# Narrowing doubles in two VectorE passes, and column sums in 64-column products

## The chip, the cores and the metric

The kernel runs on one core of a Trainium2 chip. A core has five engines that run side by side and meet through semaphores: TensorE (PE, matrix products into PSUM; its weight loads are listed as PEld), VectorE (DVE), ScalarE (ACT), GpSimd (POOL) and SyncE (SP, which here only issues transfers). The metric is the device time of one execution in microseconds; the median of the runs counts.

## The reference

Two blocks follow one another. The first is an attention with sketched polynomial features, for 4 batches, 4 heads, 1088 positions and 32 dimensions; the second is a feed-forward block with a sigmoid gate on 4352 tokens of 128 features, with 1536 hidden features.

```
phi(x):  a = x S1^T, b = x S2^T          # 8 values each
         phi = outer(a, b) as 64 features
q_p, k_p = phi(q), phi(k)
kv  = sum over s of k_p[s] v[s]^T        # 64 x 32
z   = sum over s of k_p[s]               # 64
x   = (q_p kv) / (q_p z + 1e-6)          # heads side by side: 4352 x 128

gate = sigmoid(x @ w_gate)               # 128 x 1536
out  = (gate * (x @ w_val)) @ w_out      # 1536 x 128
```

q, k and v come as 32-bit floats. [...]

## The kernel before

**Stages.** Until about 15 us the kernel builds the features of batch 0 and the first rows of x (transposed, tile `xT`). Then it goes through the tokens in chunks of 512 (`tok_chk`, nine chunks, the last of 256). For each chunk, `w1` makes one "wave" per block j of 128 hidden features (12 blocks, `NJ`): two products of `xT` with w_gate and w_val (line 501), a sigmoid on ScalarE (line 509) and, one slot later, the multiplication `g` on VectorE (line 540). `w2` (line 382) sums chunk 0 through w_out; chunks 1 to 7 use a scheme of seven half-size products (`w2_a`, `w2_b`, line 338) that needs sums of g, made by GpSimd (line 328). The attention of batches 1 to 3 is woven between the waves.

**Order.** All engines but SP follow an order written out by hand: instructions go to each engine's queue in the order of the program. `slot(group, waves)` emits a group of instructions and then that many waves, each preceded by the `glu` of the wave before and by the w2 work that is due. In chunk 0, TensorE's order is wave j, the output sum of block j−1, wave j+1, and so on.

**Narrowing.** A double is loaded as two 32-bit words, `lo` and `hi`. `narrow` is a generator of four steps. Before the change they are:

- step 0: GpSimd caps `hi`, read as a float, at ±122880 (line 97, tile `cap`); ScalarE scales `lo` to a small integer (line 101, tile `tail`);
- step 1: VectorE shifts and masks (line 105), then combines with the sign bits (line 109), giving `head`;
- step 2: ScalarE squares `cap` (line 117), into a PSUM bank of the pool `pso` where one is free; GpSimd adds `tail` to `head` as integers (line 118);
- step 3: VectorE multiplies `head` by "square is at least a threshold" (line 127), which sends tiny numbers to zero, and writes the weight into `w_sb`.

`narrow_01(part, step)` does this for blocks 0 and 1: part 0 and part 1 are gate and value of blocks 0 and 1, and part 2 is w_out of both, each of 256 columns. `narrow_w(j, step)` does blocks 2 to 11, each of 384 columns. The steps of a block are spread over the waves of chunk 0: the wave of block j emits step 3 of block j+1, steps 1 and 2 of block j+2, and step 0 of block j+4. S1 and S2 go through the same steps in a small tile of 16 partitions, at the start.

**The head.** Before the first wave: `turn_k` transposes k, `st` transposes S, `kps` and `ab` (lines 630 and 737) multiply k and q with S, `kab` (line 640) turns the result, `outer` (line 709) forms the features, `kv0` sums them with v, `dn(0, 0, rest)` makes denominators (line 1020) and numerators (line 1039), and `divide` writes `xT` (line 1060) in two parts of 256 tokens. Between them stand `warm` products of ones (line 260), whose results nobody reads. In `divide`, `between=head1` is emitted after the first transposed reciprocal `rb` (line 1070) and ahead of the first xT part.

**Denominators of batches 1 to 3.** `den_j` (line 978) makes `PD` in SBUF; `den_i` (line 991) sums it over i with a 0/1 mask of 32 columns per head, in four products; `turn_den` transposes the result (line 1003).

Of the kernel before, what the change touches and what calls it, by code (L numbers as in the profile page):

```python
# [8 lines left out]
F32 = mybir.dt.float32  # L9
I32 = mybir.dt.int32  # L10
U32 = mybir.dt.uint32
I64 = mybir.dt.int64
ALU = mybir.AluOpType
ACTF = mybir.ActivationFunctionType
MUL = ALU.mult

P = 128
# [3 lines left out]
def kernel(  # L21
# [12 lines left out]
    nc = tc.nc  # L34

    B, H, S, D = q.shape
# [4 lines left out]
    NJ = DFF // P  # L41
# [10 lines left out]
    const = ctx.enter_context(tc.tile_pool(name="const", bufs=1))  # L52
# [9 lines left out]
    pso = ctx.enter_context(tc.tile_pool(name="pso", bufs=1, space=bass.MemoryType.PSUM))  # L62
# [17 lines left out]
    wide = S1.dtype == I64  # L80
    assert all((a.dtype == I64) == wide for a in (S2, moe_w_gate, moe_w_val, moe_w_out))

    def narrow(out, bits, eng, bank=None, copies=None):

        p, n, m = bits.shape[:3]
        lo, hi = bits[:, :, :, 0].bitcast(U32), bits[:, :, :, 1]

        def tmp(dt, tag, bufs):
            return sbN.tile([P, 3, P], dt, tag=tag, name=tag, bufs=bufs)[:p, :n, :m]

        cap, tail = tmp(I32, "cap", 6), tmp(I32, "tail", 5)
        eng.tensor_scalar(
            out=cap.bitcast(F32), in0=hi.bitcast(F32), scalar1=122880.0, scalar2=-122880.0,
            op0=ALU.min, op1=ALU.max,
        )  # L100
        nc.scalar.activation(out=tail, in_=lo, func=ACTF.Copy, scale=2.0**-29)
        yield

        head = tmp(I32, "head", 3)
        nc.vector.tensor_scalar(  # L105
            out=head, in0=cap, scalar1=3, scalar2=0x3FFFFFF8,
            op0=ALU.logical_shift_left, op1=ALU.bitwise_and,
        )
        nc.vector.scalar_tensor_tensor(  # L109
            out=head, in0=cap, scalar=-0x40000000, in1=head, op0=ALU.bitwise_and, op1=ALU.bitwise_or  # L110
        )
        yield
        square = cap.bitcast(F32)
        if bank:
            square = pso.tile([P, 512], F32, tag=bank, name="square")[:, : n * m]
            square = square.rearrange("p (n m) -> p n m", n=n)
        nc.scalar.activation(out=square, in_=cap.bitcast(F32), func=ACTF.Square)
        nc.gpsimd.tensor_tensor(out=head, in0=head, in1=tail, op=ALU.add)  # L118
        yield

        head = head.bitcast(F32)
        if copies:
            square, head = (
                bass.AP(tensor=x.tensor, offset=x.offset, ap=[list(x.ap[0]), [0, copies], [1, m]])
                for x in (square, head)
            )
        nc.vector.scalar_tensor_tensor(  # L127
            out=out, in0=square, scalar=1.265625 * 2.0**-30, in1=head, op0=ALU.is_ge, op1=MUL
        )
        yield  # L130


    s4 = const.tile([2 * R, 4, D], F32, tag="s4", name="s4")
    s_in = const.tile([2 * R, 1, D, 2], I32, tag="s_in", name="s_in") if wide else s4[:, :1]
# [10 lines left out]
    w_sb = const.tile([P, 3, NJ, P], F32, tag="w_sb", name="w_sb")  # L145
    HALF = TCH // 2
    ws = const.tile([P, 4, NJ // 2, 64], F32, tag="ws", name="ws")
    w_in = {}
# [26 lines left out]
    narrowing = {}  # L175

    def narrow_w(j, step):
        if not 0 <= j < NJ:
            return
        n, jj = divmod(j, 2)  # L180
        if wide:
            if step == 0:
                narrowing[j] = narrow(
                    w_sb[:, :, j, :], w_in[n][:, :, jj], nc.gpsimd, "acc1" if j < NJ - 2 else None
                )
            next(narrowing[j])


    def narrow_01(part, step):
        if wide:  # L190
            if step == 0:
                i = (slice(0, 2), part) if part < 2 else (2, slice(0, 2))
                narrowing["01", part] = narrow(
                    w_sb[:, i[0], i[1]],
                    w_in[0][:, i[0], i[1]],
                    nc.gpsimd,
                    "acc0" if part else "acc1",
                )
            next(narrowing["01", part])


# [53 lines left out]
    def warm(*cols):  # L255
        t = psm.tile([P, 2, 512], F32, tag="wave", name="warm")
        x = nc.const_aps.tensor(1.0, [P, P], F32)
        for n in cols:
            r = nc.const_aps.tensor(1.0, [P, n], F32)
            nc.tensor.matmul(out=t[:, 0, :n], lhsT=x, rhs=r, start=True, stop=True)  # L260
# [18 lines left out]
    for c in range(2):  # L279
        rows = slice(64 * c, 64 * c + 64)  # L280
        nc.vector.tensor_reduce(
            out=m_col[rows, c],
            in_=ident[rows].rearrange("p (k j) -> p j k", j=R),
            axis=mybir.AxisListType.X,
            op=ALU.add,
        )
    for t, x in (
# [5 lines left out]
        out=e_sum,  # L293
        in_=bass.AP(
            tensor=e_row.tensor,
            offset=e_row.offset,
            ap=[list(e_row.ap[0]), [0, 2], [1, R], [0, R]],
        ),
    )
    eps = const.tile([P, 1], F32, tag="eps")  # L300
    nc.gpsimd.memset(eps, 1e-6)
    zb = const.tile([P, H, 32], F32, tag="zb", name="zb")
    nc.gpsimd.memset(zb, 0.0)
    nc.gpsimd.memset(v_sb[64:, :, 0], 0.0)
# [310 lines left out]
    KP, QP, BQ, ND, KAB, ASB, KVZ, KVD, Z4, ZS, A8, B8, ZW, PD, RC = ({} for _ in range(15))  # L615

    WD = 160
    mask = {}
# [248 lines left out]
    def kvd(b):  # L867
        KVD[b] = sbA.tile([P, 2, 2, F], F32, tag="kvd", name="kvd")
        k0 = KVZ[b][:, : 2 * F]
        n = 2 if b > 0 else 1  # L870
        nc.scalar.copy(
            out=KVD[b][:, :n],
            in_=bass.AP(
                tensor=k0.tensor, offset=k0.offset, ap=[list(k0.ap[0]), [F, n], [0, 2], [1, F]]
            ),
        )
# [19 lines left out]
    def ndt(b):  # L896
        if b == 0:
            t = pso.tile([P, TCH], F32, tag="acc0", name="ndps")
            ndps = t.rearrange("p (w x) -> p w x", w=2)
        else:  # L900
            ndps = ps2.tile([P, 2, 512], F32, tag="two", name="ndps")[:, 0].rearrange(
                "p (w x) -> p w x", w=2
            )
        if b == 0:
            nc.tensor.matmul(
                out=ndps[:, 0, :P],
                lhsT=KVD[b][:, 0].rearrange("p c f -> p (c f)"),
                rhs=ident,
                is_transpose=True,
                start=True,  # L910
                stop=True,
            )
        for c in range(2 if b else 0):
            nc.tensor.matmul(
                out=ndps[64 * c : 64 * c + 64, 0, :P],
                lhsT=KVD[b][:, 0, c],
                rhs=ident,
                start=True,
                stop=True,
            )  # L920
        ND[b] = sbA.tile([P, P], F32, tag="nd", name="nd")
        nc.scalar.copy(out=ND[b], in_=ndps[:, 0, :P])
# [64 lines left out]


    def den_i(b, dps):
        for h in range(H):  # L990
            nc.tensor.matmul(
                out=dps[32 * h : 32 * h + 32],
                lhsT=mask["head"][:, h % 2, :],
                rhs=PD[b][:, h // 2, :],
                start=True,
                stop=True,
            )
        return dps
# [85 lines left out]
        return divide  # L1084

    if wide:
        steps = narrow(s4, s_in, nc.vector, copies=4)
        for _ in range(3):
            next(steps)
    turn_k(0, 0, KBASE[2] + 1)  # L1090
# [2 lines left out]
    else:  # L1093
        nc.vector.tensor_copy(
            out=s4[:, 1:],
            in_=bass.AP(
                tensor=s4.tensor, offset=s4.offset, ap=[list(s4.ap[0]), [0, 3], [1, D]]
            ),
# [5 lines left out]
        out=st_[:, : 2 * R],  # L1104
        lhsT=s4.rearrange("p g d -> p (g d)"),
        rhs=ident[: 2 * R, : 2 * R],
# [1 line left out]
        start=True,  # L1108
        stop=True,
    )  # L1110
    warm(256)
    st_ = st_[:, : 2 * R].rearrange("p (n r) -> p n r", n=2)
    sk = const.tile([P, 2, 2, R], F32, tag="sk")
    nc.vector.tensor_tensor(
        out=sk,
        in0=bass.AP(
            tensor=st_.tensor, offset=st_.offset, ap=[list(st_.ap[0]), [0, 2], [R, 2], [1, R]]
        ),
        in1=bass.AP(
            tensor=hm.tensor, offset=hm.offset, ap=[list(hm.ap[0]), [R, 2], [0, 2], [1, R]]  # L1120
        ),
        op=MUL,
# [6 lines left out]
    for n, inner in enumerate(([[1, R], [0, R]], [[0, R], [1, R]])):  # L1129
# [3 lines left out]
            out=t, in_=bass.AP(tensor=s0.tensor, offset=s0.offset, ap=[list(s0.ap[0])] + inner)  # L1133
# [23 lines left out]
    def rest(turn, rc, dT):  # L1157
        kv0([1, 2, 3, 4, 0])
        for pi in range(2):
            outer(0, pi, 5, NJK - 1)  # L1160
        kv0(range(5, NJK))
        turn()
        nt = rc.shape[1] - 1
        nc.scalar.activation(out=rc[:, :nt], in_=dT[:, :nt, :2], func=ACTF.Identity, bias=eps)
        kvd(0)
        narrow_01(0, 1)
        narrow_01(0, 2)
        ndt(0)

    divide = dn(0, 0, rest)  # L1170
    warm(256)

    def head1():
        narrow_01(1, 1)
        narrow_01(0, 3)
        narrow_01(1, 2)
        narrow_01(2, 0)
        narrow_w(2, 0)

    divide((0, 4), (4, 8), between=head1)  # L1180
    narrow_01(1, 3)
    narrow_01(2, 1)
    narrow_01(2, 2)

# [174 lines left out]
```

## Time and profile before

| what | us |
|---|---|
| median of 3 runs | 293.81 |
| lowest and highest | 293.73 and 299.78 |
| the profiled execution | 294.1 |
| its span, first to last instruction | 292.3 |
| TensorE busy | 286.5 |
| VectorE busy | 188.8 |
| GpSimd busy | 162.7 |
| ScalarE busy | 92.1 |

The span is shorter than the time by 1.8 us, which lie around it. An engine counts as busy while one of its instructions runs. In a timeline a line has the start, the duration, the engine, the line of the program, the operation, output and inputs, and in brackets how long the engine had been idle and what it had waited for. TensorE computes a 32-bit product in two instructions.

### The profile page before, as it was taken

What the parts mean: (1) busy time and instruction counts of PE and PEld (TensorE: products, weight loads), DVE (VectorE), ACT (ScalarE), POOL (GpSimd) and SP (SyncE); (2) the same over time, 40 slices, a digit from 0 to 9 for tenths busy, and PEclk for the clock granted to TensorE, in tenths of its full rate; (3) what the DMA queues carried; (4) which work ended last, traced back from release to release, by engine and by line L of the source; (5) the groups of instructions that cost most, each with busy time, mean ns of one, the idle gap of its engine ahead of it and who ended that gap; (6) DMA issues with size and microseconds to landing.
All of it is one profiled execution on the core that took longest, in us unless ns stands there. A gap on an engine that the chain in (4) does not pass through costs nothing.

```text
span 292.3 us, 5784 instructions
## 1 busy us (share of the span) xinstructions
PE 286.5 (98%) x2276; PEld 154.9 (53%) x2276; DVE 188.8 (65%) x320; ACT 92.1 (32%) x168; POOL 162.7 (56%) x221
## 2 busy tenths in 40 slices
PE   8899999999999999999999999999999999999995
PEld 4444433345455455554555555554555555555895
DVE  6998789985837866677556685668336423642482
ACT  3557542322323222323233213423233222322421
POOL 2365644896646558546446597664465555656300
PEclk9999999999999999999999999999999999999999
DMA  7994522374720187506000584202000200010002
GB/s 216 336 354 87 147 70 84 109 185 111 239 33 0 30 195 148 147 7 183 8 0 2 153 151 108 36 2 37 0 2 0 36 2 0 0 30 8 2 2 54
DMA packets 28890, 24.23 MB, mean 83 GB/s; under 512 B 18560, under 2 KB 24064, under 8 KB 28864
## 3 DMA queue, kind: packets, MB, share of 16 engines
q1 hardware_dynamic: 25808, 21.95, 29.6%
q10 hardware_dynamic: 3056, 1.92, 2.3%
q8 instruction: 18, 0.29, 0.4%
q14 instruction: 8, 0.07, 0.1%
HBM read 20.60 MB, written 3.26 MB: 82 GB/s over the span
## 4 chain that ended last, share of the span: by engine, by line
PE 85%; DMA 6%; DVE 3%; POOL 2%; SPq 1%; issue 1%; ACT 0%; POOLq 0%; ACTq 0%
PE wave L501 55%; PE prod L338 22%; DMA v<-in_v_dram 3%; POOL head L118 2%; DMA w_in<-in_moe_w_out_dram 2%; PE moeout L408 2%; PE moeout L382 1%; PE kvz L849 1%; DVE w_sb L127 1%; DVE head L109 1%; DMA kq<-in_k_dram 1%; PE nps L1214 1%; SPq L157 1%; DVE head L105 1%; PE kps L630 1%
## 5 line engine op out<-in xcount | busy, mean ns | idle before, releaser
L501 PE MATMUL wave<-xT,w_sb 128*64 128x512 f32 (+3 forms) x820 | 210.6, 566 | 0.1
L501 PEld LDWEIGHTS wave<-xT,w_sb 128*64 128x64 f32 (+1 forms) x820 | 85.2, 140 | 63.4 <-issue 49.5
L540 DVE TENSOR_TENSOR g<-wave,sg 128x512 f32<-128x512 f32 x96 | 65.9, 686 | 77.3 <-ACT sg L509 76.2
L509 ACT ACTIVATE sg<-wave 128x512 f32<-128x512 f32 x102 | 61.0, 598 | 170.5 <-PE wave L501 161.0
L328 POOL TENSOR_TENSOR tsum<-g 128x256 f32<-128x256 f32 x84 | 68.1, 813 | 25.6 <-DVE g L540 25.2
L328 POOL TENSOR_TENSOR tsum<-g,tsum 128x256 f32<-128x256 f32 x42 | 35.2, 839 | 59.5 <-DVE g L540 59.2
L338 PE MATMUL prod<-tsum,ws 128*64 128x256 f32 x252 | 62.8, 381 | 0.0
L338 PEld LDWEIGHTS prod<-tsum,ws 128*64 128x64 f32 x252 | 31.2, 136 | 16.8 <-issue 12.4
L338 PE MATMUL prod<-g,w_sb 128*64 128x256 f32 x168 | 34.9, 383 | 0.0
L328 POOL TENSOR_TENSOR tsum<-tsum,g 128x256 f32<-128x256 f32 x42 | 32.9, 782 | 3.3
L338 PEld LDWEIGHTS prod<-g,w_sb 128*64 128x64 f32 x168 | 15.7, 136 | 18.2 <-issue 15.4
L338 PE MATMUL prod<-tsum,w_sb 128*64 128x256 f32 x84 | 25.3, 383 | 0.0
L338 PE MATMUL prod<-g,ws 128*64 128x256 f32 x84 | 25.0, 379 | 0.0
L118 POOL TENSOR_TENSOR head<-head,tail 128x384 int32<-128x384 int32 (+2 forms) x14 | 13.3, 953 | 17.9 <-DVE head L109 11.5
L338 PEld LDWEIGHTS prod<-g,ws 128*64 128x64 f32 x84 | 11.5, 137 | 3.7
L382 PE MATMUL moeout<-g,w_sb 128*128 128x512 f32 (+1 forms) x28 | 12.6, 607 | 0.3 <-DVE w_sb L127 0.3
L338 PEld LDWEIGHTS prod<-tsum,w_sb 128*64 128x64 f32 x84 | 10.8, 137 | 2.4 <-issue 1.9
L709 DVE TENSOR_TENSOR kp<-kab 128x1152 f32<-128x1152 f32 (+2 forms) x10 | 10.9, 1103 | 0.0
L829 DVE TENSOR_TENSOR qp<-qp,bq 128x1152 f32<-128x1152 f32 (+1 forms) x7 | 9.5, 1353 | 1.9 <-DMA a<-dq 1.1
L533 DVE TENSOR_TENSOR g<-wave,sg 128x512 f32<-128x512 f32 x6 | 6.8, 1138 | 4.5 <-ACT sg L509 4.5
L440 DVE TENSOR_TENSOR res<-prod,other 64x512 f32<-64x512 f32 (+1 forms) x14 | 7.6, 544 | 3.0 <-ACT other L434 3.0
L475 DVE STREAM_TRANSPOSE o_sb<-res 64x512 f32<-64x512 f32 x14 | 9.6, 690 | 0.0
(121 smaller groups left out, 203.0 us busy)
## 6 DMA issues: line engine op xcount, KB each, us to landing
qp<-dq SPq DMA_DIRECT2D x7, 576.0 KB
bq<-dq SPq DMA_DIRECT2D x14, 288.0 KB
kq<-in_k_dram SPq DMA_DIRECT2D x3, 544.0 KB
kq<-in_q_dram SPq DMA_DIRECT2D x3, 544.0 KB
w_in<-in_moe_w_out_dram SPq DMA_DIRECT2D x6, 256.0 KB
w_in<-in_moe_w_gate_dram SPq DMA_DIRECT2D x5, 256.0 KB
w_in<-in_moe_w_val_dram SPq DMA_DIRECT2D x5, 256.0 KB
v<-in_v_dram SPq DMA_DIRECT2D x8, 144.0 KB
```

What stands on the lines that cost most here:

```text
L118: nc.gpsimd.tensor_tensor(out=head, in0=head, in1=tail, op=ALU.add)
L328: nc.gpsimd.tensor_tensor(out=t[:, u], in0=in0, in1=in1, op=ALU.subtract)
L338: nc.tensor.matmul(out=out, lhsT=lhsT, rhs=rhs, start=start, stop=stop, skip_group_check=True)
L382: nc.tensor.matmul(out=moe["acc"][d], lhsT=w_sb[:, 2, j, d], rhs=g[:, jj], start=(j == 0), stop=(j == NJ - 1),)
L440: nc.vector.tensor_tensor(out=out, in0=in0, in1=in1, op=op)
L475: nc.vector.transpose(out=o_sb[:64, d].rearrange("p t x -> p (t x)"), in_=r[:, 1 + 2 * d : 3 + 2 * d].rearrange("p u x -> p (u x)"),)
L501: nc.tensor.matmul(out=wv[d, which, jj * tw + o : jj * tw + o + tp], lhsT=w_sb[:, which, j0 + jj, d], rhs=xT[:, t0 + o : t0 + o + tp], sta ...
L509: nc.scalar.activation(out=sg, in_=wv[:, 0], func=ACTF.Sigmoid)
L533: nc.vector.tensor_tensor(out=g.rearrange("p (j u s y) -> p j y u s", j=2, u=2, y=4), in0=wv[:, 1].rearrange("p (j y u s) -> p j y u s", j ...
L540: nc.vector.tensor_tensor(out=g, in0=wv[:, 1], in1=sg, op=MUL)
L709: eng.tensor_tensor(out=KP[b][:, pi, j0:j1].rearrange("p j m (i l) -> p (j m) i l", i=R), in0=bass.AP(tensor=a0.tensor, offset=a0.offset, ...
L829: nc.vector.tensor_tensor(out=q0, in0=q0, in1=half(BQ[b], n), op=MUL)
```

## The change

Weights are narrowed by other operations. ScalarE takes the magnitude of `hi` (Abs), and GpSimd clamps it in place between 2^-15 and 122880. ScalarE makes `tail` as a float near 2.0 (Identity with a scale and a bias tile). VectorE shifts the magnitude left by three in one pass; GpSimd adds the bits of `tail` as a wrapping integer sum; VectorE takes the sign bit from the raw word `hi` and combines it with the sum in a second pass. The square, its PSUM bank and the third VectorE pass are gone. S1 and S2 keep the old steps (`narrow_copies`). The tiles `head` are now allocated in step 0.

In the head, steps 1 of parts 0 and 1 follow each other, and so do their steps 2; both parts' step 3 now stands in `head1`, ahead of the first xT part. One warm product has 64 columns instead of 256. `den_i` sums in two products of 64 columns instead of four of 32.

```diff
+    def narrow(out, bits):
+        tmp, lo, hi = pieces(bits)
+        cap, tail, head = tmp(I32, "cap", 6), tmp(F32, "tail", 5), tmp(I32, "head", 3)
+        mag = cap.bitcast(F32)
+        nc.scalar.activation(out=mag, in_=hi.bitcast(F32), func=ACTF.Abs)
+        nc.gpsimd.tensor_scalar(
+            out=mag, in0=mag, scalar1=2.0**-15, scalar2=122880.0, op0=ALU.max, op1=ALU.min
+        )
+        nc.scalar.activation(out=tail, in_=lo, func=ACTF.Identity, bias=two, scale=2.0**-51)
+        yield
+        nc.vector.tensor_scalar(
+            out=head, in0=cap, scalar1=3, scalar2=None, op0=ALU.logical_shift_left
+        )
+        yield
+        nc.gpsimd.tensor_tensor(out=head, in0=head, in1=tail.bitcast(I32), op=ALU.add)
+        yield
+        nc.vector.scalar_tensor_tensor(
+            out=out.bitcast(I32),
+            in0=hi,
+            scalar=-0x80000000,
+            in1=head,
+            op0=ALU.bitwise_and,
+            op1=ALU.bitwise_or,
+        )
+        yield
...
+    two = const.tile([P, 1], F32, tag="two_", name="two_")
+    nc.gpsimd.memset(two, 2.0)
...
     def den_i(b, dps):
-        for h in range(H):
+        for pi in range(2):
             nc.tensor.matmul(
-                out=dps[32 * h : 32 * h + 32],
-                lhsT=mask["head"][:, h % 2, :],
-                rhs=PD[b][:, h // 2, :],
+                out=dps[64 * pi : 64 * pi + 64],
+                lhsT=mask["head"].rearrange("p m x -> p (m x)"),
+                rhs=PD[b][:, pi, :],
                 start=True,
                 stop=True,
             )
...
-    warm(256)
+    warm(64)
...
         kvd(0)
         narrow_01(0, 1)
+        narrow_01(1, 1)
         narrow_01(0, 2)
+        narrow_01(1, 2)
         ndt(0)
...
     def head1():
-        narrow_01(1, 1)
         narrow_01(0, 3)
-        narrow_01(1, 2)
+        narrow_01(1, 3)
         narrow_01(2, 0)
         narrow_w(2, 0)
 
     divide((0, 4), (4, 8), between=head1)
-    narrow_01(1, 3)
     narrow_01(2, 1)
     narrow_01(2, 2)
```

## The prediction

> **What bounds the kernel now.** I read the table by stretches first, since a mean over the whole span hides the stage that the change touches.
>
> ```profile
> core 0: us, PE busy (x) PEld busy (x) DVE busy (x) ACT busy (x) POOL busy (x), PEclk, DMA share, GB/s
> 0.00:15.28 15.28, 13.16 (x196) 6.33 (x197) 12.28 (x38) 6.56 (x18) 4.86 (x19) 1.00 0.93 280
> 15.28:42.40 27.12, 26.71 (x93) 11.58 (x93) 22.55 (x44) 15.08 (x30) 16.21 (x22) 1.00 0.54 152
> 52.00:292.30 240.30, 237.07 (x1952) 133.42 (x1933) 145.01 (x224) 68.14 (x116) 138.12 (x176) 1.00 0.26 61
> ```
>
> TensorE is busy all through. The weights are narrowed between 10 and 46 us, so the last 240 us hold nothing of the change but the sums over i. In the middle stretch VectorE looks loaded too (22.55 of 27.12). Is narrowing or TensorE the pace there? The timeline of that stretch answers it (columns: start, duration, engine, line):
>
> ```profile
> 27.85 0.56 DVE L127 SCALAR_TENSOR_TENSOR w_sb<-square,head 128x384 f32<-128x384 f32 x1 [0.60 <-POOL head L118]
> 28.32 0.35 DVE L105 TENSOR_SCALAR head<-cap 128x384 int32<-128x384 int32 x1
> 28.71 0.56 DVE L109 SCALAR_TENSOR_TENSOR head<-cap,head 128x384 int32<-128x384 int32 x1
> 28.83 1.88 PE L501 MATMUL wave<-xT,w_sb 128*128 128x512 f32 x4
> 29.44 1.00 POOL L118 TENSOR_TENSOR head<-head,tail 128x384 int32<-128x384 int32 x1 [1.12 <-DVE head L109]
> 30.47 0.56 DVE L127 SCALAR_TENSOR_TENSOR w_sb<-square,head 128x384 f32<-128x384 f32 x1 [0.60 <-POOL head L118]
> 31.41 1.88 PE L501 MATMUL wave<-xT,w_sb 128*128 128x512 f32 x4
> ...
> 39.68 1.35 DVE L829 TENSOR_TENSOR qp<-qp,bq 128x1152 f32<-128x1152 f32 x1
> 41.09 0.69 PE L1020 MATMUL dps<-qp,zb 128*32 128x288 f32 x8
> ```
>
> Waves start 2.58 us apart, which is what TensorE needs: six instructions (four of a wave, two of the output sum) of 0.43 us. The narrowing is a ring: last pass L127, mask passes L105 and L109, GpSimd's add L118, and the next L127 waits for that add. It turns in 30.47 − 27.85 = 2.62 us, 0.04 slower than TensorE, and so far it only eats slack: TensorE never stops between 23.7 and 40.85 us. **Thus two passes instead of three cannot buy 0.56 us per block; it can only buy the gaps around the loop.** One gap is at the end: L829 is queued behind L109, and TensorE, free at 40.85, begins the denominators at 41.09. The other is at the start:
>
> ```profile
> 17.20 0.73 POOL L118 TENSOR_TENSOR head<-head,tail 128x256 int32<-128x256 int32 x1 [0.88 <-DVE head L109]
> 17.33 1.01 DVE L109 SCALAR_TENSOR_TENSOR head<-cap,head 128x384 int32<-128x384 int32 x1
> 18.86 0.41 DVE L127 SCALAR_TENSOR_TENSOR w_sb<-square,head 128x256 f32<-128x256 f32 x1
> 19.33 1.12 PE L382 MATMUL moeout<-g,w_sb 128*128 128x512 f32 x2 [0.34 <-DVE w_sb L127]
> ```
>
> TensorE is through with the first two waves at 15.28 + 8 × 0.43 = 18.72 and starts the output sum at 19.33, when the w_out block is narrowed: 0.6 us lost. See also that L109 took 1.01 instead of 0.56 beside an add of GpSimd.
>
> Before the first wave the path runs over VectorE:
>
> ```profile
> 5.52 0.99 PE L260 MATMUL warm<-const-float32-1.0 128*128 128x256 f32 x2
> 6.45 0.72 PE L630 MATMUL kps<-kT,sk 64*32 64x288 f32 x16
> 7.20 0.85 DVE L640 STREAM_TRANSPOSE kab<-kps 128x288 f32<-128x288 f32 x2 [0.76 <-PE kps L630]
> 14.81 0.41 DVE L1060 TENSOR_TENSOR xT<-nps,rb 128x256 f32<-128x256 f32 x1
> ```
>
> kps waits for neither kT (done 5.70) nor sk (done 5.82) but for the warm product in front of it; VectorE then sits 0.76 us, and from 7.20 to the first xT at 14.81 it has hardly a gap. For the sums over i:
>
> ```profile
> 75.91 0.48 PE L991 MATMUL nps<-pd,head 128*32 128x160 f32 x8
> 76.31 0.65 PE L338 MATMUL prod<-g,w_sb 128*64 128x256 f32 x4
> ```
>
> The eight instructions hold TensorE for 0.40 us, three times in the kernel.
>
> [...] The old last pass took one input from PSUM and kept 0.56 beside GpSimd's clamp; the new one has two SBUF inputs. [...] The trace shows one table load for Sigmoid, Copy, Square and Identity; it has no Abs. [...]
>
> **Part by part.**
>
> (1) *Warm product of 64 columns.* Two instructions at 0.46 us (5.52 to 6.44) become two weight loads of 0.25 and little else, ended by about 5.9. kps can start about 5.95, 0.50 earlier, and VectorE's chain from L640 with it. v and the first weights have landed by 10.07, where the first tail started; the shifted chain wants them at 10.95 and 11.9. So −0.50 at the transposed denominators (12.00 to 11.50). [...]
>
> (2) *Head order.* After dT: two shifts of 0.28 (before: shift and mask, 0.28 + 0.34). Then reciprocal, rb, and now both last passes before xT, each with two SBUF inputs. GpSimd's adds run 12.4 to 13.1 and 13.1 to 13.8, so the first last pass, ready at 13.2, is locked out until 13.8 and the second starts 14.15, or 14.5 if the w_out clamp slips between. xT then starts at 14.48 to 14.83, against 14.81. Middle: 14.65, a gain of 0.15 out of the 0.50.
>
> (3) *Join with the output sum.* Counted from xT: g of wave 0 waits for its sigmoid, at +3.12 instead of +3.45, as both mask passes (0.34 and 0.93) are gone. The last pass of the w_out block is then ready at +3.72; GpSimd's clamp for block 3, now behind an Abs that ends about +3.55, holds the port from about +3.6 to +4.13. So the pass ends about +4.5 and the sum begins at +4.60, against 19.33 − 14.81 = +4.52: a loss of 0.08. If the pass comes first: +4.2, a gain of 0.3.
>
> (4) *The ring, twelve blocks.* Gone: L109 (0.47 of ring). New: the last pass may wait for the clamp (0.53). Worst ring: 0.47 + 0.35 + 0.17 (hand-over) + 0.96 + 0.53 = 2.48; without the lock 2.02. Both are under TensorE's 2.58, so the pace stays and the gain is nothing. [...] The clamp's new wait for Abs holds only the clamp: behind it on GpSimd stands an add that VectorE's later shift feeds anyway. The new last pass isn't in the trace: 0.56 (L109, same inputs but dense) to 0.93 (the locked L127 at 44.88); I take 0.56 plus the lock. The shift with one operation: 0.35 as L105; I see no reason for less.
>
> (5) *End of the loop.* The ring has slack, so L829 starts about 1 us earlier against TensorE and ends before wave 9 does. The denominators then follow at the 0.09 switch instead of 0.24: −0.15. The later gap of 0.17 (47.61 to 47.78, waiting for g) shrinks to a switch: −0.1 (0 to −0.15).
>
> (6) *Sums over i.* 160 columns take 2 × 0.43 × 160/512 = 0.27 us either way: four narrow tiles side by side, or two. But 64-column tiles are the mode of the products that follow, so one of two switches goes: −0.1 each (0 to −0.13), three times: −0.3. Nothing hides TensorE there, nor does the next wave wait for anything else.
>
> (7) PSUM squares gone, another memset: 0.1 us on an idle GpSimd; no path.
>
> Sum: −0.15 + 0.08 − 0.25 − 0.3 = **−0.6 us**. The profiled execution took 294.1 (span 292.3, 1.8 around it), 0.3 above the median of 293.81; −0.6 gives 293.5 there and **293.2** against the median. A measurement of this kernel tells about 2% from no change (5.9 us), so this is "within 2%".
>
> **Rivals.**
> - *The start is worth what it promises* (0.20). The clamps lose both races for the port: xT 14.48 (−0.33), join −0.3. With −0.55 from (5) and (6): −1.2, 292.6. For it: VectorE's idle 0.76 before L640 is real. Against: GpSimd reaches its clamp first wherever the old loop shows them side by side (27.78 before 27.85).
> - *Slower: the clock* (0.18). [...]
> - *Abs isn't in the sigmoid table* (0.02). [...]
>
> The forecast has 0.60, alone 292.7 to 293.6. The range of 292.3 to 294.2 leaves out most of the slow clock and the tables. Faster by over 2% follows from none of the cases (0.01 for what I overlooked), slower from the tables alone (0.02).
>
> **What would show it.** Right: waves in the loop still 2.58 apart, VectorE busy down from 188.8 by 3 to 7 us (7.3 of L109 gone, less what the lock adds), kps near 5.95, no gap before L1020, den_i followed by the product after about 0.3 us. Step (2) is wrong if xT starts outside 14.4 to 14.9, step (3) if the output sum starts over 4.7 after xT. The whole is wrong if wave-to-wave distance grows, if more than one table load appears, or if gaps open after 52 us.

## The result and the profile after

| | before | after |
|---|---|---|
| median of 22 runs each, us | 294.33 | 295.41 |
| the profiled execution, us | 294.1 | 295.0 |
| its span, us | 292.3 | 293.2 |
| busy us: TensorE, VectorE, GpSimd, ScalarE | 286.5, 188.8, 162.7, 92.1 | 286.0, 185.9, 174.3, 93.2 |

The 22 runs of before take in the three shown earlier; their median is 0.5 above that of the three. The ratio of after to before is 1.0046, with a 95% interval from 1.0027 to 1.0065. The ratios in this document leave out the few runs in a slower state (299 us and more here), so they are not quotients of the two medians. The change made the kernel slower by about half a per cent. The forecast was 0.6 us faster, 293.2 us in a range of 292.3 to 294.2; measured is 1.1 us slower. The sign was wrong, and moving the range up by the 0.5 would not take in 295.41 either.

VectorE lost 2.9 us of work, just under the 3 to 7 that the prediction named, but GpSimd gained 11.6 us. The stretch around the wave loop shows where. This is the table by stretches of the changed kernel (length, then busy time of each engine), cut at the same instructions as the one shown of before, as near as the shift allows:

```profile
0.00:15.48 15.48, 12.86 (x197) 6.25 (x197) 12.63 (x37) 7.11 (x19) 7.47 (x21) 1.00 0.92 278
15.48:43.78 28.30, 26.96 (x93) 11.34 (x93) 20.80 (x35) 16.11 (x31) 25.64 (x21) 1.00 0.55 153
53.30:293.20 239.90, 236.66 (x1940) 133.96 (x1921) 144.66 (x224) 68.15 (x116) 137.99 (x176) 1.00 0.27 62
```

Both kernels have 93 TensorE instructions in the middle stretch. It grew from 27.12 to 28.30 us, while GpSimd's busy time there (the fifth figure after the length) went from 16.21 to 25.64 us in about as many instructions (22 and 21). One of its instructions must be much longer. The groups with their shapes name it. First the old clamp, from the profile of before (columns: count, then busy us and mean ns of one, then idle time ahead of it):

```profile
L97 POOL TENSOR_SCALAR cap<-w_in 128x384 f32<-128x384 f32 x10 | 5.3, 537 | 0.0
L97 POOL TENSOR_SCALAR cap<-w_in 128x256 f32<-128x256 f32 x3 | 1.2, 409 | 0.0
```

and the new one, from the changed kernel:

```profile
L99 POOL TENSOR_SCALAR cap<-cap 128x384 f32<-128x384 f32 x10 | 15.3, 1534 | 0.2 <-ACT cap L98 0.2
L99 POOL TENSOR_SCALAR cap<-cap 128x256 f32<-128x256 f32 x3 | 3.3, 1095 | 0.2
```

Same engine, same operation name, same shape, two limits in both: yet 1534 ns instead of 537. It is no longer hidden. The chain of waits of the changed kernel, within 23 to 32 us, runs through it (columns: start, duration, what):

```profile
24.37 1.00 POOL head L108
25.37 2.91 POOL cap L99 x2
28.28 0.98 POOL head L108
29.26 0.02 issue
29.28 0.86 DVE w_sb L110
30.14 0.14 issue
30.28 1.96 PE wave L514 x4
```

and the timeline shows TensorE standing still there:

```profile
26.46 1.89 PE L514 MATMUL wave<-xT,w_sb 128*128 128x512 f32 x4
28.19 1.10 PE L395 MATMUL moeout<-g,w_sb 128*128 128x512 f32 x2
30.28 1.10 PE L514 MATMUL wave<-xT,w_sb 128*128 128x512 f32 x2 [0.99 <-DVE w_sb L110]
```

From wave 4 (26.46) to wave 5 (30.28) 3.82 us pass, where before 2.57 us passed (26.26 to 28.83). The next wave follows after 2.65 us, and from there on waves are 2.58 us apart again. The loss is a single one because of an irregular round: in the code the wave of block 2 emits step 0 of block 5 and of block 6, all others at most one. These are the two clamps from 25.34 to 28.29, and the add of block 5, for which wave 5 waits, stands behind both in GpSimd's queue: it starts 3.88 us after the add before it (24.37 and 28.25). With one clamp per round GpSimd turns in 1.0 + 1.5 = 2.5 us (adds at 28.25, 30.73, 33.20, 35.69, 38.17), just under TensorE's 2.58: it has no gap left, but TensorE doesn't wait for it any more. TensorE doesn't regain the lost time either: it is busy for 286.0 of 293.2 us, and at wave 9 it is 1.53 behind, after 1.45 at wave 5.

The distance between the two kernels, followed along TensorE's instructions, adds up to the 0.9 us between these two profiles (the medians are 1.1 apart):

| instruction | before | after | difference |
|---|---|---|---|
| first wave | 15.28 | 15.48 | +0.20 |
| first output sum | 19.33 | 19.54 | +0.21 |
| wave 4 | 26.26 | 26.46 | +0.20 |
| wave 5 | 28.83 | 30.28 | **+1.45** |
| wave 9 | 39.13 | 40.66 | +1.53 |
| denominators `dps` | 41.09 | 42.47 | +1.38 |
| `kps` of the next batch | 51.36 | 52.66 | +1.30 |
| wave after the first sums over i | 77.23 | 78.39 | +1.16 |
| after the second | 137.28 | 138.31 | +1.03 |
| after the third | 201.69 | 202.58 | +0.89 |
| end of the span | 292.3 | 293.2 | +0.9 |

So the first 15 us cost 0.2 in this profile, the clamp 1.25, and the waves behind it another 0.08. Everything after them brings 0.64 back: 0.15 at the end of the loop, 0.08 at the gap behind it, and 0.13 to 0.14 at each of the three sums over i.

### The profile page after: what moved, and what is told of

Read it like the earlier page. It is cut to its first block, busy times and chain, and to the rows that moved or that the text cites. A ratio compares the mean times of both kernels' runs of the same rounds, so it can differ in the third digit from the quotient of the medians.

```text
span 293.2 us, 5760 instructions
## 1 busy us (share of the span) xinstructions
PE 286.0 (98%) x2264; PEld 155.2 (53%) x2264; DVE 185.9 (63%) x307; ACT 93.2 (32%) x168; POOL 174.3 (59%) x222
## 4 chain that ended last, share of the span: by engine, by line
PE 90%; POOL 4%; DVE 2%; DMA 1%; issue 1%; ACT 1%; ACTq 0%; POOLq 0%; DVEq 0%
PE wave L514 59%; PE prod L351 22%; PE moeout L395 2%; POOL cap L99 2%; PE moeout L421 2%; POOL head L108 2%; DMA kq<-in_k_dram 1%; PE kvz L862 1%; PE nps L1227 1%; PE kps L643 1%; DVE w_sb L110 1%; PE cqps L789 0%; PE denj L991 0%; PE nps L1004 0%; DVE kp L722 0%
## 5 line engine op out<-in xcount | busy, mean ns | idle before, releaser
L553 DVE TENSOR_TENSOR g<-wave,sg 128x512 f32<-128x512 f32 x96 | 65.9, 687 | 78.0 <-ACT sg L522 76.6
L341 POOL TENSOR_TENSOR tsum<-g 128x256 f32<-128x256 f32 x84 | 67.0, 800 | 28.3 <-DVE g L553 28.1
L341 POOL TENSOR_TENSOR tsum<-g,tsum 128x256 f32<-128x256 f32 x42 | 34.2, 814 | 58.2 <-DVE g L553 57.8
L341 POOL TENSOR_TENSOR tsum<-tsum,g 128x256 f32<-128x256 f32 x42 | 34.9, 830 | 3.3
L99 POOL TENSOR_SCALAR cap<-cap 128x384 f32<-128x384 f32 (+1 forms) x13 | 18.6, 1432 | 0.4 <-ACT cap L98 0.2
L108 POOL TENSOR_TENSOR head<-head,tail 128x384 int32<-128x384 int32 (+1 forms) x13 | 12.9, 998 | 2.9 <-DVE head L104 2.5
L110 DVE SCALAR_TENSOR_TENSOR w_sb<-w_in,head 128x384 int32<-128x384 int32 (+1 forms) x13 | 10.4, 811 | 4.5 <-POOL head L108 4.5
L722 DVE TENSOR_TENSOR kp<-kab 128x1152 f32<-128x1152 f32 (+2 forms) x10 | 11.1, 1122 | 0.0
```

Of the source, the lines that this page charges most:

```text
L99: nc.gpsimd.tensor_scalar(out=mag, in0=mag, scalar1=2.0**-15, scalar2=122880.0, op0=ALU.max, op1=ALU.min)
L108: nc.gpsimd.tensor_tensor(out=head, in0=head, in1=tail.bitcast(I32), op=ALU.add)
L110: nc.vector.scalar_tensor_tensor(out=out.bitcast(I32), in0=hi, scalar=-0x80000000, in1=head, op0=ALU.bitwise_and, op1=ALU.bitwise_or,)
L341: nc.gpsimd.tensor_tensor(out=t[:, u], in0=in0, in1=in1, op=ALU.subtract)
L553: nc.vector.tensor_tensor(out=g, in0=wv[:, 1], in1=sg, op=MUL)
L722: eng.tensor_tensor(out=KP[b][:, pi, j0:j1].rearrange("p j m (i l) -> p (j m) i l", i=R), in0=bass.AP(tensor=a0.tensor, offset=a0.offset, ...
```

## The experiments

Each kernel is the changed one with the edit shown, unless its heading says otherwise. A ratio is to the kernel before, run on the same chip, with its 95% interval.

**Does the order of the two limits make the clamp slow?** The old clamp took the minimum first, the new one the maximum. The first run only swaps them.

```diff
-            out=mag, in0=mag, scalar1=2.0**-15, scalar2=122880.0, op0=ALU.max, op1=ALU.min
+            out=mag, in0=mag, scalar1=122880.0, scalar2=2.0**-15, op0=ALU.min, op1=ALU.max
```

> The changed kernel with GpSimd's clamp written as min with 122880 first and max with 2^-15 second, still in place; the values are the same. In the changed kernel this clamp took 1.49 us for 384 columns (1.07 for 256), against 0.53 (0.41) of the old one, which had min first, read the strided raw words and wrote another tile. Theory A (the order of the two operations picks a slow path on GpSimd): the clamp falls to about 0.53 and the time to about 0.5 us under the kernel before, since the 1.25 us that wave 5 waits go. Theory B (working in place is slow): the clamp stays at 1.49 and the time within 0.2 us of the changed kernel, about 1.1 over the kernel before. Theory C (the bound 2^-15, or the dense source, is slow): as B.

Measured: 293.49 us against 294.19, ratio 0.9979 [0.9967, 0.9992], so 0.70 faster than before. The groups of this run:

```profile
L99 POOL TENSOR_SCALAR cap<-cap 128x384 f32<-128x384 f32 x10 | 5.2, 521 | 3.5 <-ACT cap L98 3.5
```

and its timeline of TensorE:

```profile
26.04 1.88 PE L514 MATMUL wave<-xT,w_sb 128*128 128x512 f32 x4
28.61 1.88 PE L514 MATMUL wave<-xT,w_sb 128*128 128x512 f32 x4
31.18 1.88 PE L514 MATMUL wave<-xT,w_sb 128*128 128x512 f32 x4
```

The clamp is back at 0.52 us and the waves are 2.57 apart throughout. The order of the two operations alone decides, and with the fast order the change as a whole gains about what the forecast had.

**Or is it the in-place write, or the data from ScalarE?** The Abs writes a tile of its own, the clamp reads it and writes `cap` (now in 4 buffers instead of 6); maximum still first.

```diff
+        src = tmp(F32, "src", 2)
-        nc.scalar.activation(out=mag, in_=hi.bitcast(F32), func=ACTF.Abs)
+        nc.scalar.activation(out=src, in_=hi.bitcast(F32), func=ACTF.Abs)
-            out=mag, in0=mag, scalar1=2.0**-15, ...
+            out=mag, in0=src, scalar1=2.0**-15, ...
```

> The changed kernel with Abs writing a tile of its own (two buffers; the tile cap has four instead of six to make room), so that the clamp is not in place; max first as in the changed kernel. Theory B (in place is slow): clamp 0.53, time about 0.5 us under the kernel before. Theory A (order) and C (bound or dense source): clamp 1.49, time about 1.1 over the kernel before.

Measured: 295.50 us, ratio 1.0038 [1.0022, 1.0055]; the clamp took 1532 ns, and TensorE again waited 0.98 us before wave 5. Writing in place is not the cause. The data still come from ScalarE here; the next run has them straight from the load.

**The same swap in the kernel before.** If the order is the cause, it must slow the old code as well, which has neither Abs nor an in-place clamp.

```diff
 # kernel before
-            scalar1=122880.0, scalar2=-122880.0, op0=ALU.min, op1=ALU.max,
+            scalar1=-122880.0, scalar2=122880.0, op0=ALU.max, op1=ALU.min,
```

> The kernel before, with only its cap on GpSimd written as max with -122880 first and min with 122880 second. Theory A (order): its cap goes from 0.53 to about 1.5 us; GpSimd's round is then 2.5 of 2.58 us with two caps in one round once, so the kernel loses 1 to 2 us. Theories B and C: cap 0.53, time as the kernel before within 0.2 us.

Measured: 298.31 us, ratio 1.0149 [1.0118, 1.0179]. The groups and the timeline of this run:

```profile
L97 POOL TENSOR_SCALAR cap<-w_in 128x384 f32<-128x384 f32 x10 | 15.2, 1522 | 0.0
```

```profile
20.60 1.13 PE L382 MATMUL moeout<-g,w_sb 128*128 128x512 f32 x2 [1.47 <-DVE w_sb L127]
31.53 1.13 PE L382 MATMUL moeout<-g,w_sb 128*128 128x512 f32 x2 [0.82 <-DVE g L540]
```

So the same swap makes the old clamp as slow, and the order of the two operations is the cause in both kernels. The old kernel pays 4.1 us for it (298.31 less 294.19), the new one about 2 (1.0046 less 0.9979, of 294). In the old one TensorE waits at the first output sum (1.47 here, 0.34 before), and from wave 2 to wave 5 another 2.6 us go (21.57 to 32.69, against 20.29 to 28.83 before), over half of it at the double round (two clamps from 28.04 to 31.05). It has three VectorE passes in its ring. That two passes are what gives the new narrowing more room against a slow clamp fits with this, but is not shown apart from the rest of the change.

**What the clamp costs in all.** This kernel leaves the clamp out, so values outside the limits come out wrong.

```diff
-        nc.gpsimd.tensor_scalar(
-            out=mag, in0=mag, scalar1=2.0**-15, scalar2=122880.0, op0=ALU.max, op1=ALU.min
-        )
```

> The changed kernel without GpSimd's clamp; it only bears on magnitudes under 2^-127 or over 2^129. It shows what the rest of the change is worth, whatever makes the clamp slow. Theory 'the clamp alone turned the sign': no wait of 1 us before wave 5, waves 2.58 apart from the third on, no lock-out of the last pass by a clamp; 0.6 to 1.0 us under the kernel before. Rival 'the lost time lies elsewhere (the head, ScalarE's longer round, the port)': still over the kernel before, by 0.3 us or more.

Measured: 292.78 us, ratio 0.9952 [0.9936, 0.9968]. Even the fast clamp isn't quite free: this run is 0.7 below the one with the minimum first, although the two intervals just touch. A part of that is seen at the first output sum, which came 4.21 us after the first xT here (18.86 and 14.65) and 4.48 after it there.

**Which operations are slow?** Three runs, with a single time each, change the clamp's operations. The first keeps only the maximum, so large values aren't capped; the second adds 2^-15 instead of taking the maximum; the third keeps only the minimum.

```diff
 # maximum only
-            scalar1=2.0**-15, scalar2=122880.0, op0=ALU.max, op1=ALU.min
+            scalar1=2.0**-15, scalar2=None, op0=ALU.max
 # add, then minimum
-            scalar1=2.0**-15, scalar2=122880.0, op0=ALU.max, op1=ALU.min
+            scalar1=2.0**-15, scalar2=122880.0, op0=ALU.add, op1=ALU.min
 # minimum only
-            scalar1=2.0**-15, scalar2=122880.0, op0=ALU.max, op1=ALU.min
+            scalar1=122880.0, scalar2=None, op0=ALU.min
```

> The changed kernel whose clamp has only the lower bound (one operation, max with 2^-15); the upper one bears only on weights over 2^129. If max as such is slow on GpSimd, the clamp takes 1.0 us or more for 384 columns. If only the pair max-then-min misses a fast path, it takes about 0.5, as with min first.

> The changed kernel whose clamp adds 2^-15 and then takes the minimum with 122880, so it leaves out the lower bound and shifts the magnitudes by 2^-15. If two operations in one pass are slow in general and min-then-max alone is fast, the pass takes about 1.5 us for 384 columns; if max in first place is what is slow, about 0.5.

> After, with a clamp of one operation, the minimum with 122880; the lower bound is left out, so tiny weights are not kept from wrapping. With max alone the pass over 384 columns took 1.17 us, with min then max 0.51. If the fast path is bound to the operation that comes first (min): about 0.5 us and waves 2.58 apart, time as with min first (293.5). If a single operation is slower whatever it is, and only the pair min then max has a fast form: about 1.17 us, time about 293.9 as with max alone.

The groups, in this order, one fence for each run:

```profile
L99 POOL TENSOR_SCALAR cap<-cap 128x384 f32<-128x384 f32 x10 | 11.6, 1167 | 0.4 <-ACT cap L98 0.2
```

```profile
L99 POOL TENSOR_SCALAR cap<-cap 128x384 f32<-128x384 f32 x10 | 15.3, 1533 | 0.0
```

```profile
L99 POOL TENSOR_SCALAR cap<-cap 128x384 f32<-128x384 f32 x10 | 11.8, 1182 | 0.5 <-ACT cap L98 0.5
```

One operation alone takes 1.17 to 1.18 us, whichever of the two it is; another pair takes 1.53; of all that were tried only the minimum followed by the maximum takes 0.52, less than half of either operation by itself. So it isn't the maximum that is slow: this one pair is fast. The traces also show where a long clamp begins to hurt. With 1.17 the adds on both sides of the double round are 3.24 us apart (23.29 and 26.53 with the maximum alone), and the waves of that run stay 2.57 to 2.58 apart; with the slow pair they are 3.88 apart (24.25 and 28.13), and TensorE waits 0.99 us before wave 5, as in the changed kernel. The single times fit: 293.89 us with the maximum and 293.53 with the minimum, 295.86 with the slow pair, against 294.52, 294.29 and 294.52 of the kernel before. No run spreads the two clamps over two rounds. Why the pair is fast inside GpSimd is left open: no trace shows inside the instruction.

**The steps that looked right: warm product.** From here on the base has the minimum first. The warm product goes back to 256 columns.

```diff
-    warm(64)
+    warm(256)
```

> The changed kernel with min first in the clamp (which was 0.70 us under the kernel before), and the warm product back at 256 columns. Prediction's step (1): kps starts about 6.45 instead of 6.15, the first wave up to 0.3 later, the time up to 0.3 us longer than with 64 columns, so about 0.4 under the kernel before. Rival 'the warm product is hidden, kps waits for sk behind kT's second half': first wave and time unchanged within 0.1.

Measured: 293.58 us, ratio 0.9980 [0.9972, 0.9989], against 0.9979 with 64 columns. The times can't tell the two apart. In the traces kps starts at 6.67 with 256 columns and at 6.15 with 64, the first wave at 15.47 and 15.09. But the transfer of k had also landed later in the long one (VectorE waited for it until 5.54, and started at 5.12 in the short one), so the pair isn't a clean comparison. This step stays inconclusive in time.

**The sums over i.** Four products of 32 columns again.

```diff
-        for pi in range(2):
+        for h in range(H):
             nc.tensor.matmul(
-                out=dps[64 * pi : 64 * pi + 64],
-                lhsT=mask["head"].rearrange("p m x -> p (m x)"),
-                rhs=PD[b][:, pi, :],
+                out=dps[32 * h : 32 * h + 32],
+                lhsT=mask["head"][:, h % 2, :],
+                rhs=PD[b][:, h // 2, :],
```

> The changed kernel with min first in the clamp, and the sums over i back in four products of 32 columns. Prediction's step (6): TensorE holds the sums 0.40 us instead of 0.32 and the next wave starts 0.1 to 0.14 later, three times, so 0.3 to 0.4 us more: about 0.3 under the kernel before. Rival 'the wait is made up elsewhere': no change of the time.

Measured: 293.66 us, ratio 0.9980 [0.9966, 0.9994]; 0.17 more than with two products, inside both intervals, so the time shows neither the gain nor the rival. The trace has what the time can't resolve: the first products of 64 columns follow 0.41 us after the sums here (75.40 to 75.81) and 0.32 after them with two (76.04 to 76.36). The edit changes two things, the width of the tiles and the number of products, so it doesn't tell which of them costs the 0.09.

**The order in the head.** Blocks 0 and 1 take their steps as in the kernel before: one last pass before xT, the other behind it.

```diff
         narrow_01(0, 1)
-        narrow_01(1, 1)
         narrow_01(0, 2)
-        narrow_01(1, 2)
         ndt(0)
...
     def head1():
+        narrow_01(1, 1)
         narrow_01(0, 3)
-        narrow_01(1, 3)
+        narrow_01(1, 2)
         narrow_01(2, 0)
...
+    narrow_01(1, 3)
     narrow_01(2, 1)
```

> The changed kernel with min first in the clamp, and the old order of the first three blocks in the head (block 1's shift after the first transposed reciprocal, its last pass after both xT parts). Theory 'the new order pays with the port' (both last passes stand ahead of xT, locked out by GpSimd's adds): xT starts earlier by up to 0.3 (14.3 instead of 14.63), and the time falls by as much unless the w_out block then comes later. Rival 'the new order helps': the first output sum starts later than 19.11, and the time rises by 0.2 or more.

Measured: 293.32 us, ratio 0.9971 [0.9958, 0.9985]. VectorE's timeline of this run:

```profile
13.32 0.42 DVE L110 SCALAR_TENSOR_TENSOR w_sb<-w_in,head 128x256 int32<-128x256 int32 x1
14.28 0.42 DVE L1073 TENSOR_TENSOR xT<-nps,rb 128x256 f32<-128x256 f32 x1 [0.54 <-PE nps L1052]
```

With one pass ahead of it, VectorE is free at 13.74 and xT waits for TensorE's numerators. With both (13.21 to 14.70 in the base) xT comes at 14.63. Counted from the transposed denominators, xT starts 2.59 us after them here and 2.89 there: the new order costs 0.3 us ahead of xT. The two passes took 1.49 us in the base, beside GpSimd's adds (12.44 to 13.85) and its clamp (14.03 to 14.43); the single pass here, at 13.32 between two adds, took 0.42. In time the difference is 0.17, within the intervals.

**Which goes first at the first output sum, the clamp or the last pass?** ScalarE makes `tail` ahead of the magnitude, so that GpSimd's clamp comes later than VectorE's last pass.

```diff
+        nc.scalar.activation(out=tail, in_=lo, func=ACTF.Identity, bias=two, scale=2.0**-51)
         nc.scalar.activation(out=mag, in_=hi.bitcast(F32), func=ACTF.Abs)
         nc.gpsimd.tensor_scalar(
             out=mag, in0=mag, scalar1=122880.0, scalar2=2.0**-15, op0=ALU.min, op1=ALU.max
         )
-        nc.scalar.activation(out=tail, in_=lo, func=ACTF.Identity, bias=two, scale=2.0**-51)
```

> The changed kernel with min first in the clamp, and ScalarE making the tail before the magnitude, so that each clamp starts some 0.6 us later on GpSimd. Prediction's step (3) says that the last pass of the w_out block is locked out by block 3's clamp (18.27 to 18.78 against a pass ready at 18.36). Lock theory: the pass now comes first, the first output sum starts 0.2 to 0.3 us earlier against xT (4.2 instead of 4.48), and the time falls by as much, to about 0.95 under the kernel before. Rival 'the pass waits for GpSimd's add or for the wave itself': the start stays at 4.4 to 4.5 after xT and the time does not change.

Measured: 292.96 us, ratio 0.9956 [0.9939, 0.9973]. First the base, minimum first, then the run with the tail first:

```profile
18.27 0.51 POOL L99 TENSOR_SCALAR cap<-cap 128x384 f32<-128x384 f32 x1 [0.22 <-ACT cap L98]
18.36 1.16 DVE L110 SCALAR_TENSOR_TENSOR w_sb<-w_in,head 128x256 int32<-128x256 int32 x2
19.11 1.13 PE L395 MATMUL moeout<-g,w_sb 128*128 128x512 f32 x2 [0.30 <-DVE w_sb L110]
```

```profile
18.07 0.89 DVE L110 SCALAR_TENSOR_TENSOR w_sb<-w_in,head 128x256 int32<-128x256 int32 x2
18.51 0.81 POOL L100 TENSOR_SCALAR cap<-cap 128x384 f32<-128x384 f32 x1 [0.40 <-ACT cap L99]
18.54 1.12 PE L395 MATMUL moeout<-g,w_sb 128*128 128x512 f32 x2
```

The VectorE line joins two passes, the w_out block and the longer one of block 2 behind it; the sum waits for the first alone. In the base the clamp is 0.09 us ahead, and the first pass takes 0.69, both 1.16. With the tail first the passes go ahead, take 0.42 and together 0.89, and the clamp is stretched to 0.81 instead. The sum starts 4.20 us after xT (14.34) instead of 4.48, and TensorE doesn't wait. So at this place the one that came second took longer, the pass by 0.27 us or the clamp by 0.30. But the added time is not the whole length of the other instruction. In the wave loop the last pass comes 0.07 us behind a clamp, in the base and in the changed kernel:

```profile
23.21 0.50 POOL L99 TENSOR_SCALAR cap<-cap 128x384 f32<-128x384 f32 x1
23.28 0.85 DVE L110 SCALAR_TENSOR_TENSOR w_sb<-w_in,head 128x384 int32<-128x384 int32 x1
```

```profile
29.21 1.55 POOL L99 TENSOR_SCALAR cap<-cap 128x384 f32<-128x384 f32 x1
29.28 0.85 DVE L110 SCALAR_TENSOR_TENSOR w_sb<-w_in,head 128x384 int32<-128x384 int32 x1 [1.17 <-POOL head L108]
```

It takes 0.85 in both, 0.29 more than alone (0.56, at 42.48 in the changed kernel), and beside the long clamp it ends 0.6 us before the clamp does. Why the long clamp adds no more than the short one is open.

Ahead of xT the tail-first run gains in the same way: the two last passes took 1.25 us instead of 1.49, and xT followed the transposed denominators after 2.64 instead of 2.89. The two places make 0.53 us in the traces. The median fell by 0.53 as well, but the ratios say 0.7 and their intervals overlap, so the times bear out no more than the direction.

**Both together.** Tail first and the old order in the head.

> After, with the clamp's minimum first, ScalarE's tail ahead of its magnitude, and the old order of blocks 0 and 1 in the head (one step each ahead of the numerators, the rest behind). If the two gains are independent: against the run with the tail first (1.4 under before), the old order lets the first xT part wait for nps alone, about 0.3 us earlier than with both last passes ahead of it, so about 292.7 for 294.3 before, ratio about 0.9947. If the tail-first order already has what the old head order gains (with it, xT came at 14.34, hardly later than the 14.28 of the old order): about 293.0, ratio 0.9956. The output sum should start xT + 4.2 in both; the waves stay 2.58 apart.

Measured: 293.35 us against 294.29, ratio 0.9967 [0.9954, 0.9980]. The gains do not add: the ratio is no better than with the tail first alone (0.9956 [0.9939, 0.9973]). The trace tells why. xT came at 14.16, but the sum 4.46 after it:

```profile
17.28 1.01 POOL L108 TENSOR_TENSOR head<-head,tail 128x384 int32<-128x384 int32 x1 [0.30 <-DVE head L104]
17.91 1.44 DVE L110 SCALAR_TENSOR_TENSOR w_sb<-w_in,head 128x256 int32<-128x256 int32 x2
18.62 1.12 PE L395 MATMUL moeout<-g,w_sb 128*128 128x512 f32 x2 [0.28 <-DVE w_sb L110]
```

With xT earlier, the last pass is ready earlier too and runs into block 2's add, which ends at 18.29, instead of the clamp. The two passes took 1.44 us there, 0.89 with the tail first alone. So the lowest time of the kernels that keep the clamp has the minimum first and the tail first: faster than before by 0.3 to 0.6%, and faster than the change as made by 0.9% (0.9956 against 1.0046). Its interval overlaps those of the other kernels with the minimum first, so the times don't rank them.

## Why the prediction was wrong

**Step (4), the ring, is the step that failed.** It said "the last pass may wait for the clamp (0.53)", and gave the "worst ring" as 2.48. The 0.53 was read off the old L97, as the nearest row, without a range, although the two operations of the new clamp stand in the other order. The clamp measured 1.53. The step let it bear on the ring in one way only, as a lock that holds VectorE up. No run shows a lock or a port by itself; what the runs showed is a last pass that took 0.29 longer (0.85 less 0.56) beside the long clamp and beside the short one. What it did not add up at all is the clamp as work in GpSimd's queue, ahead of the next add. GpSimd's round is 1.0 + 1.53 = 2.5 us for one clamp, still under TensorE's 2.58, so a pure rate argument would have found no loss even with the right duration. It was the double round, 3.88 us from add to add, that cost 1.25 us. It was to be seen beforehand: the code has a wave that emits two steps 0, and in before the two clamps take 1.03 us in one piece. With 0.53 each they were harmless; the account of the order ahead of the prediction ("step 0 of block j+4") left them out.

The rest of step (4) held. The tail with its bias tile took 0.64 us and the Abs 0.55; with the sigmoid's 0.60 that is 1.79 of a round of 2.58. The changed kernel has one table load (1.28 us), as the one before has, so the rival with the tables did not come. One sum is off without consequence: the same terms without the lock make 1.95, not 2.02.

The two orders differ per column, not by a fixed amount. From 256 to 384 columns the fast pair goes from 0.40 to 0.51 us, which is 0.86 ns per column; the other order of the same two operations goes from 1.07 to 1.49, 3.3 ns per column.

**Step (1), warm product: right in kind in the traces, smaller and unsteady.** kps was to start at 5.95. It started at 6.41 in the profile of after, and between 5.82 and 6.15 in eight other traces with 64 columns. Two things that the step took as fixed vary. The second half of k landed late in after, where VectorE waited for it:

```profile
5.56 0.71 DVE L612 STREAM_TRANSPOSE kT<-kq 128x512 f32<-128x512 f32 x1 [0.26 <-DMA kq<-in_k_dram]
6.20 0.15 DVE L1127 TENSOR_TENSOR sk<-st,hm 128x32 f32<-128x32 f32 x1
6.41 0.72 PE L643 MATMUL kps<-kT,sk 64*32 64x288 f32 x16 [0.45 <-DVE sk L1127]
```

So with the warm product out of the way, k's landing is the next wait in line in this profile. Nor does all of it arrive: with the tail first kps came at 5.94, 0.51 earlier than before, and the transposed denominators at 11.70, only 0.30 earlier; the pass over kp ahead of them (L722) took 1.21 us there and 1.02 before. And the short product itself took 0.43 us in some traces, 0.69 in others. The rival with the slow clock did not decide in after, where kps held TensorE 0.72 us, as before, at a granted clock of 1.00 in the first 15 us of both. But it isn't empty: in three of those eight traces kps held TensorE longer, 0.94 us (no clamp, maximum only) and 1.02 (add then minimum). VectorE then got kps's result at 7.14 to 7.23, against 7.20 before, so there the step gained nothing. Why kps took longer there is not shown. The trace of before has two rates: instructions of 512 columns start 0.85 us apart at first (1.76, 2.61, 3.46) and 0.43 apart in the waves, and after the last short warm product's first instruction the second starts 0.59 later (5.52, 6.11), kps 0.34 after that. No run shows what sets the lower rate or ends it.

**Step (2), a right sum from wrong parts; step (3), right with the fast clamp.** With the fast clamp xT came at 14.63, where 14.65 was said. But the gain ahead of it was 0.26 (transposed denominators at 11.74, not 11.50), and the new order cost 0.08 against before's 2.81, not the 0.35 that the step took off the 0.50. That the two errors cancel is luck. The step took an add of GpSimd to hold a last pass back until its end, which no run shows as such; what the traces showed is 1.46 to 1.49 us for the two passes beside the adds and a clamp, and 0.42 for a pass alone. The join was to be +4.60, or +4.2 if VectorE came first. With the minimum first it was +4.48, with the parts that the step names: g at +3.12, the last pass ready at +3.73, the clamp ahead of it at +3.64. With the tail first it was +4.20. The +4.53 of after is near the number for another reason: the pass there ran into block 2's add (18.20 to 19.20), and the clamp came only behind it.

**Steps (5) and (6), right.** From wave 9 to the denominators 1.96 us passed before and 1.81 after: 0.15, as said, and L829's counterpart started 0.96 us earlier against wave 9 (40.25 with 40.66, 39.68 with 39.13 before), where about 1 was said. The later gap gave 0.08 for 0.1. The sums over i gave 0.13 to 0.14 each for 0.1: the products follow them after 0.32 us instead of 0.40:

```profile
77.21 0.49 PE L1004 MATMUL nps<-pd,head 128*64 128x160 f32 x4
77.53 0.60 PE L351 MATMUL prod<-g,w_sb 128*64 128x256 f32 x4
```

The next wave came 1.18 us after the sums began (78.39) and 1.32 before (75.91 to 77.23). The 0.09 and the −0.1 each were meant as the cost of a switch of tile width. No run shows such a switch by itself. What the traces showed in its place: between the estimated end of a wave (22.01, four instructions of 0.43 from 20.29) and the `cqps` at 22.10 lie 0.09 before, and as much between wave 9 (estimated to end at 42.38) and the denominators at 42.47 after. At the sums over i the number of products changed with the width, so the 0.08 there can't be given to either.

**The total.** −0.6 was forecast. With the clamp's order put right, −0.70 was measured (about −0.6 by the ratio). So the rest of the working stood, part of it by errors that cancelled by luck, and one price and the queue behind it turned the sign. The rival on the slower side, the clock, is not what slowed the kernel (the granted clock is 1.00 in every stretch of both tables); none of the rivals had GpSimd as the engine that becomes the bound, although its clamp had a new form, as the last pass had, which was bounded from both sides.

## What to carry to other kernels

A row prices an instruction only if everything in it is the same, the order of its operations included (here 0.52 against 1.53 us); where a change swaps two operations, the price is unknown and needs both ends, however harmless the swap looks in arithmetic. For an engine in the background, add up its queue for the worst round, not for the mean one: a round with two of an instruction can stop the bound engine once, and what TensorE, busy all through, lost there it did not get back. Where an instruction of one engine takes longer beside one of another (here the last pass, 0.85 against 0.56 us), try swapping the producers that decide which comes first; here that brought 0.5 us in the traces, beside the 0.7 that the change with the fast clamp measured.

## What the runs showed of the hardware

- On GpSimd a `tensor_scalar` over 128 × 384 fp32 took 0.52 us with minimum then maximum, 1.53 with maximum then minimum, 1.53 with add then minimum, and 1.17 to 1.18 with the minimum or the maximum alone. Here two operations took less than either of them alone.
- A VectorE pass with two SBUF inputs over 128 × 384 took 0.56 us alone and 0.85 close behind a GpSimd clamp, whether that clamp lasted 0.50 or 1.55 us.
- When a transfer lands differs between runs, and it reached TensorE. The run with the minimum first waited on VectorE until 72.42 us for a transfer (`bq`), and TensorE then lost 0.36 us at the next batch's numerators; in the run with four sums the same instruction began at 71.78, and TensorE had no such wait. The line below is the base's. Between kernels this close (medians of 293.49 and 293.66 us) read shifts between neighbouring instructions, and not the spans of single profiles (292.0 and 291.8).

```profile
74.96 1.16 PE L1227 MATMUL nps<-qp,nd 64*32 64x512 f32 x32 [0.36 <-DVE g L553]
```
